# Pinning the first layer's matmuls in traced order, and maxima two to three plan steps behind their VectorE part

## The chip, the cores and the metric

The kernel runs on one core of one Trainium2 chip. The metric is the device time of one execution in microseconds, the median of several runs. Beside the runs stands one profiled execution, from which all rows below are taken.

## The reference

Chunked attention feeds two expert layers. In float32:

```python
# attention: 4 batches x 8 heads x 768 positions x 64; chunks of 32 queries see
# 16 positions to the left, 8 to the right and 8 memory slots (64 keys in all)
scores = scale * np.matmul(q_c, k_full.transpose(0, 1, 3, 2))
a = np.exp(scores - np.max(scores, axis=-1, keepdims=True))
a = a / (np.sum(a, axis=-1, keepdims=True) + 1e-09)
out[:, :, c_start:c_end] = np.matmul(a, v_full)
...
x = np.ascontiguousarray(attn_out.transpose(0, 2, 1, 3)).reshape(B * S, H * D)   # 3072 x 512
h = x @ w_in                                        # first layer: 512 -> 2048
g = np.maximum(h, 0.0) + alpha * np.minimum(h, 0.0)
x = g @ w_out                                       # 2048 -> 512
h = x @ w2_in                                       # second layer
return (h * (1.0 / (1.0 + np.exp(-1.702 * h)))) @ w2_out
```

## The kernel before

**Numbers.** Each float32 operand is scaled by a power of two and split into a high and a low half of 16 bits. A product is three matmuls (high x high, high x low, low x high). The scales come from absolute maxima. `all_max` takes a column of maxima per partition, spreads it over the partitions with a float32 matmul against the identity (the tile `mx`, L119), and reduces the result on DVE (`ar`, L120).

**First layer.** The 3072 tokens are 12 blocks of 256 (b0 to b11). The 2048 hidden units are 8 pairs of 128. A `step` handles one block and one pair: `mlp_g1` issues 24 matmuls into the tile `h` (L575) from the block's input `xt`; `mlp_act` makes the leaky ReLU of it with ACT (`t`, L610) and DVE (`gf`, L613); `mlp_split` makes the 16-bit halves `g` (L127 on ACT, L130 on DVE); four steps later `mlp_g2` issues 24 matmuls into `acc` (L655). There are 96 steps, and 4 more steps of filling. Between the parts of a step `run_plan` carries out what a table of times has due: three plan steps are one step of the layer.

**Attention.** The attention of block b is planned ahead of the steps of that block, from a list `ATT` with offsets. Its matmuls are QK0 and QK1 (`att_qk`, 16 matmuls each, L477 and L478, into the three banks `sps`), and PV0 and PV1 (`att_pv`, 48 small matmuls each, L543, into banks 0 and 1 of `sps`). QK1 overwrites what QK0 wrote once ACT has copied it out (`att_ext`, L494). After PV0, ACT casts the high half of `xt` out of the bank (`att_xhi`, L127) and DVE the low half (`att_xlo`, L130), and the same after PV1. When q, k and v are loaded, ACT takes the absolute maxima of k and q (`att_max`; the tile `junk`, L326), and DVE that of v. In the text, "PV1 of b10" is the one of the attention of block 10.

**Second layer.** Its weights are prepared in the same plan (`w_max`, `w_all`, `w_scale`, `w_dec_a`, ...), its inputs by `y_evac`, `y_max`, `y_unit`. It runs from about 720 us on.

**Order.** The program's trace is a list of instructions in the order of the code. A scheduler with a timeline of its own then decides, for each engine, in which order that engine's queue holds them, within their dependencies. An engine starts its instructions in the order of its queue. A call `tc.keep_in_program_order(x)` ties x behind the instruction traced before it on its engine. Before the change it is used for two instructions of each attention block only (the split of v, L127 and L130).

Of the kernel before, what the change touches and what calls it, by code (L numbers as in the profile page):

```python
# [36 lines left out]
def kernel(  # L37
# [14 lines left out]
    nc = tc.nc  # L52
# [60 lines left out]

    def all_max(m):
        n = m.shape[1]
        r = sm_p.tile([128, 4], F32, tag="ar", name="ar")[:, 0:n]
        pt = ps.tile([128, n, 128], F32, tag="b", name="mx")
        for i in range(n):
            nc.tensor.matmul(out=pt[:, i], lhsT=m[:, i:i + 1].to_broadcast([128, 128]), rhs=eye, start=True, stop=True)  # L119
        nc.vector.tensor_reduce(out=r, in_=pt, axis=AX.X, op=ALU.max, apply_absolute_value=True)  # L120
        return r

    def absmax(o, i):
        nc.vector.tensor_reduce(out=o, in_=i, axis=AX.X, op=ALU.max, apply_absolute_value=True)  # L124
# [17 lines left out]
    wtmp = {}  # L142
# [139 lines left out]
    def bs(nb, i):  # L282
        return blk[nb][:, i:i + 1]
# [187 lines left out]
    def att_qk(nb, i):  # L471
        q1, q2 = att["q", nb]
        kt = att["k", nb]
        k0 = 0 if i == 0 else NM + 128
        for h in range(H):
            o = sps[:, h // 3, h % 3 * TW:h % 3 * TW + TW]
            nc.tensor.matmul(out=o, lhsT=q1[:, i, h], rhs=kt[:, h, k0:k0 + TW], start=True, stop=False)  # L477
            nc.tensor.matmul(out=o, lhsT=q2[:, i, h], rhs=kt[:, h, k0:k0 + TW], start=False, stop=True)  # L478

    def att_ext(nb, i):  # L480
        sc = at_p.tile([128, 9, SL], F32, tag="sc", name="sc", bufs=2)
# [51 lines left out]
    def att_pv(nb, i):  # L533
        aT = att.pop(("a", nb, i))
        if i == 0:
            xt[nb] = xt_p.tile([128, 2, KT, TB], F16, tag="xt", name="xt")
        xp = sps[:, i].rearrange("p (j t) -> p j t", j=HP)
        for j in range(HP):
            for c in range(4):
                o = xp[:, j, 32 * c:32 * c + 32]  # L540
                w = vbd[:, 4 * i + c, j].rearrange("p a (d t) -> p (a d) t", t=2)
                for n, (wt, a) in enumerate(((0, 0), (1, 0), (0, 1))):
                    nc.tensor.matmul(out=o, lhsT=w[:, :, wt], rhs=aT[:, a, j, 32 * c:32 * c + 32], start=(n == 0), stop=(n == 2))  # L543
        att["xp", nb, i] = xp

    def att_xhi(nb, i):
# [19 lines left out]
    def mlp_g1(layer, b, p):  # L566
        x = xt[b]
        hp = ps.tile([128, 2, TB], F32, tag="b", name="h")
        for e in range(2):
            w, c = wslot[p], e  # L570
            n = 0
            for (wt, xh) in TRI:
                for kk in range(KT):
                    o = kk * 256 + c * 128
                    nc.tensor.matmul(out=hp[:, e], lhsT=w[:, wt, o:o + 128], rhs=x[:, xh, kk], start=(n == 0), stop=(n == 3 * KT - 1))  # L575
                    n += 1
        return hp

# [65 lines left out]
    def mlp_g2(layer, b, p):  # L644
        g16 = gt.pop((layer, b, p))
        if layer == 0:
            first = p == 0 or b < NA and p == HF
            last = p == NP - 1 or b < NA and p == HF - 1
            if first:
                acc[layer, b] = [ps.tile([128, 512], F32, tag="b", name="acc") for _ in range(2)]  # L650
            for e in range(2):
                w = wslot[NP + p][:, :, e * 512:(e + 1) * 512]
                for dt in range(KT):
                    for n, (wt, gh) in enumerate(TRI):
                        nc.tensor.matmul(  # L655
                            out=acc[layer, b][dt // 2][:, dt % 2 * TB:(dt % 2 + 1) * TB],
                            lhsT=w[:, wt, dt * 128:(dt + 1) * 128],
                            rhs=g16[:, gh, e],
                            start=(first and e == 0 and n == 0 and dt % 2 == 0),
                            stop=(last and e == 1 and n == 2 and dt % 2 == 1),  # L660
                        )
        else:
            if p == 0:
                acc[layer, b] = [lazy["ps"].tile([128, 512], F32, tag="a", name="acc") for _ in range(3)] + [ps.tile([128, 512], F32, tag="b", name="acc")]
            lazy["left"] += 1 - lazy.pop(("side", b, p))
            w = w2o[p // 2]
            for bank, i, (gs, o) in WIN7:
                for n, (gh, wt) in enumerate(TRI):
                    nc.tensor.matmul(  # L669
                        out=acc[layer, b][bank][:, i * 256:(i + 1) * 256],  # L670
                        lhsT=g16[:, gh, gs],
                        rhs=w[:, o, wt, p % 2],
                        start=(p == 0 and n == 0 and i == 0),
                        stop=(p == NP - 1 and n == 2 and (i == 1 or bank == 3)),
                    )
# [148 lines left out]
    def at(t, fn, *a):  # L824
        plan.setdefault(t, []).append((fn, a))
# [25 lines left out]
    def split(m, p):  # L851
# [6 lines left out]
        (-89.08, alpha_prep), (-85.94, att_qk32, 0, 0), (-84.86, w_load, 0, 0), (-82.33, att_v32, 0, 1),  # L858
        (-78.47, w_load, 1, 0), (-74.28, w_max, 0, 0), (-68.89, att_ext, 0, 0), (-58.71, att_qk32, 0, 1),
        (-54.62, att_ext, 0, 1), (-47.58, att_smax, 0, 0), (-45.32, att_exp, 0, 0), (-41.66, att_sum, 0, 0),  # L860
        (-34.37, w_all, 0, 0, 1), (-33.6, w_max, 0, 1), (-31.58, w_scale, 0, 0, 1), (-28.74, att_v32, 0, 0),
        (-28.07, att_load, 1, 1), (-27.6, att_smax, 0, 1), (-26.72, w_all, 0, 1, 2), (-25.47, att_exp, 0, 1),
        (-25.16, att_ta32, 0, 0), (-24.86, w_load, 0, 4), (-23.18, w_dec_a, 0, 0), (-23.15, w_load, 1, 1),
        (-22.75, w_dec_b, 0, 0), (-22.72, w_split_a, 0, 0), (-22.23, w_scale, 0, 1, 2), (-22.07, w_load, 1, 2),
        (-21.79, att_sum, 0, 1), (-21.75, att_pv32, 0, 0), (-20.45, att_t32, 1), (-19.95, att_ta32, 0, 1),
        (-19.78, att_pv32, 0, 1), (-19.6, att_xmax, 0, 1), (-19.14, w_load, 0, 2), (-19.11, w_load, 1, 3),
        (-18.22, att_v32, 1, 1), (-17.8, w_dec_a, 0, 1), (-16.85, w_max, 0, 2), (-16.78, w_load, 0, 3),
        (-16.05, w_max, 1, 3), (-15.51, w_max, 0, 3), (-14.02, att_xmax, 0, 0), (-13.25, att_load, 2, 2),
        (-13.14, att_v32, 1, 0), (-12.97, w_all, 0, 2, 4), (-11.75, w_load, 0, 5), (-11.41, att_xall, 0),
# [20 lines left out]
        (14.26, att_smax, 2, 0), (14.44, w_dec_b, 1, 3), (14.78, att_vr, 2, 7), (14.88, w_max, 0, 5),  # L890
        (15.48, att_exp, 2, 0), (15.76, w_max, 0, 7), (16.07, w_split_a, 1, 1), (16.29, att_qk, 2, 1),
        (16.29, att_sum, 2, 0), (17.48, att_ext, 2, 1), (18.83, w_split_b, 1, 1), (18.86, att_smax, 2, 1),
        (18.99, att_vr, 2, 5), (19.25, w_all, 0, 4, 6), (19.27, w_split_a, 1, 0), (20.02, w_max, 1, 5),
        (20.61, w_split_a, 1, 2), (20.77, att_vr, 2, 6), (21.27, w_scale, 0, 4, 6), (21.31, att_vr, 2, 4),
        (22.18, att_vr, 2, 3), (23.01, att_vr, 2, 0), (23.08, w_max, 1, 7), (23.28, att_exp, 2, 1),
        (23.31, att_a16, 2, 0), (23.39, w_dec_a, 0, 4), (23.91, w_split_a, 1, 3), (24.32, att_sum, 2, 1),
        (24.48, w_dec_a, 0, 5), (24.64, w_all, 0, 6, 8), (24.68, w_split_b, 1, 3), (24.91, w_dec_b, 0, 4),
# [16 lines left out]
    for g in range(NP):  # L914
# [164 lines left out]
```

## Time and profile before

| | |
|---|---|
| runs | 1191.53, 1194.05, 1190.81 us; median 1191.53 |
| profiled execution | 1190.76 us |
| its span, first to last instruction | 1189.0 us |
| mean granted clock of TensorE | 0.954 |
| busy: PE, DVE, ACT, POOL | 91%, 72%, 53%, 54% of the span |

The profiled execution lasts 1.76 us longer than its span, and 0.77 us less than the median of the runs. PE is TensorE's matmuls; PEld its weight loads, which run beside them. Times of the trace count from the start of the span. A matmul row's duration runs to its modelled end, so that consecutive groups overlap a little: the next group starts before the last one's end.

### The profile page before, as it was taken

To read this page: it belongs to the slowest core of one execution; us is meant where nothing else is said; L and a number is where in the kernel's file an instruction comes from. 1 tells how busy PE (TensorE), PEld (TensorE's weight loads), DVE (VectorE), ACT (ScalarE), POOL (GpSimd) and SP (SyncE) were. 2 spreads that over 40 slices of the span, in tenths; PEclk is the share of its full clock that TensorE was granted. 3 is DMA by queue.
4 is the path that set the end of the run, shared out by engine and by line. 5 is a ranking of instruction groups with operands and counts; after the bars stand their busy time and mean duration, and the time that the engine had idled before them with its cause. 6 is when DMAs were issued, how large, how long until landed. Compare 5 with 4: busy or idle time off the path is not lost.

```text
span 1189.0 us, 25654 instructions
## 1 busy us (share of the span) xinstructions
PE 1078.8 (91%) x10294; PEld 956.7 (80%) x10294; DVE 854.6 (72%) x1509; ACT 632.8 (53%) x968; POOL 637.4 (54%) x740
## 2 busy tenths in 40 slices
PE   3676779988999887999899999989999999999998
PEld 3665668877888776887788988878888888888887
DVE  6898985659787777858698634787676767667662
ACT  4567555556766475756665632545444444443442
POOL 1244542318756456617562811787685676666672
PEclk8678889999899999999899999999999999999999
DMA  9969227576989678887965390640110202000001
GB/s 207 305 126 192 90 72 160 91 145 181 238 207 262 137 203 164 235 156 191 186 191 139 102 351 19 266 169 19 56 44 6 76 19 80 21 6 14 19 19 37
DMA packets 250536, 154.53 MB, mean 130 GB/s; under 512 B 201200, under 2 KB 221680, under 8 KB 249392
## 3 DMA queue, kind: packets, MB, share of 16 engines
q1 hardware_dynamic: 250416, 152.88, 50.3%
q8 instruction: 81, 1.33, 0.5%
q14 instruction: 39, 0.32, 0.1%
HBM read 91.96 MB, written 38.93 MB: 110 GB/s over the span
## 4 chain that ended last, share of the span: by engine, by line
PE 51%; DVE 19%; DMA 11%; POOL 5%; issue 5%; ACT 4%; SPq 4%; ACTq 0%; DVEq 0%; POOLq 0%
PE acc L669 17%; PE x L586 16%; PE h L575 8%; PE acc L655 8%; DVE g L130 3%; DVE gf L613 2%; DMA q<-q 2%; POOL ga L620 2%; DMA wbig<-in_moe_w_in_dram 2%; DVE wr L198 1%; DVE wmax L124 1%; DMA w<-in_moe_w_in_dram 1%; DVE wr L199 1%; DVE blk L124 1%; DMA vbd<-in_v_dram 1%
## 5 line engine op out<-in xcount | busy, mean ns | idle before, releaser
L620 POOL TENSOR_TENSOR ga<-ga 128x128 f32<-128x128 f32 x384 | 213.1, 579 | 170.7 <-DVE ga L618 158.6
L575 PE MATMUL h<-xt,wbig 128*128 128x256 f16 x2304 | 279.6, 279 | 22.8 <-ACT xt L127 17.0
L655 PE MATMUL acc<-g,wbig 128*128 128x256 f16 x2304 | 280.5, 280 | 8.9 <-DVE yf L685 4.0
L575 PEld LDWEIGHTS <-wbig 128*128 128x128 f16 x2304 | 230.4, 100 | 55.4 <-issue 24.5
L655 PEld LDWEIGHTS <-wbig 128*128 128x128 f16 x2304 | 229.7, 100 | 41.5 <-issue 8.9
L669 PE MATMUL acc<-w2o,g 128*128 128x256 f16 x2016 | 231.7, 274 | 4.0 <-ACT g L127 3.6
L586 PE MATMUL x<-yt,w2i 128*128 128x256 f16 x2016 | 229.9, 273 | 1.0 <-DVE ha L596 0.9
L669 PEld LDWEIGHTS <-g 128*128 128x128 f16 x2016 | 197.7, 98 | 28.9 <-ACT g L127 4.5
L586 PEld LDWEIGHTS <-w2i 128*128 128x128 f16 x2016 | 197.3, 98 | 24.2 <-issue 1.4
L130 DVE SCALAR_TENSOR_TENSOR g<-ga,gk,g 128x896 f16<-128x896 f32 x96 | 121.0, 1266 | 91.2 <-ACT g L127 90.9
L127 ACT ACTIVATE g<-ga,gk 128x896 f16<-128x896 f32 x96 | 99.0, 1038 | 96.0 <-POOL ga L620 87.0
L613 DVE SCALAR_TENSOR_TENSOR gf<-t,oma,h 128x256 f32<-128x256 f32 x192 | 83.5, 473 | 76.9 <-ACT t L610 76.9
L130 DVE SCALAR_TENSOR_TENSOR g<-gf,gk,g 128x512 f16<-128x512 f32 x81 | 80.5, 994 | 20.2 <-ACT g L127 20.0
L610 ACT ACTIVATE t<-h 128x512 f32<-128x512 f32 x96 | 56.7, 591 | 70.0 <-PE h L575 46.3
L803 POOL TENSOR_TENSOR o<-o 128x256 f32<-128x256 f32 x77 | 74.3, 979 | 10.0 <-ACT o L798 9.5
L617 ACT ACTIVATE ga<-ha,l2t 128x512 f32<-128x512 f32 x48 | 34.5, 718 | 80.7 <-DVE ha L598 80.7
L228 POOL TENSOR_TENSOR wt<-wr 128x512 f32<-128x512 f32 x16 | 24.0, 1499 | 81.1 <-DVE wr L205 81.0
L214 POOL TENSOR_TENSOR wbig<-wr,wbig 128x1024 f16<-128x1024 f32 x16 | 35.1, 2202 | 53.4 <-ACT wbig L209 53.4
L127 ACT ACTIVATE g<-gf,gk 128x512 f16<-128x512 f32 x81 | 57.7, 712 | 0.5 <-DVE gf L613 0.4
L494 ACT COPY sc<-sps 32x504 f32<-32x504 f32 (+2 forms) x112 | 56.2, 502 | 1.0
L618 DVE SCALAR_TENSOR_TENSOR ga<-ga,ha 128x512 f32<-128x512 f32 x48 | 35.6, 741 | 21.0 <-ACT ga L617 21.0
L543 PE MATMUL sps<-aT,vbd 128*128 128x32 f16 x960 | 27.5, 179 | 22.7 <-DVE xt L130 16.3
(194 smaller groups left out, 1514.7 us busy)
## 6 DMA issues: line engine op xcount, KB each, us to landing
yt_dr<-yh SPq DMA_DIRECT2D x42, 256.0 KB
yt<-yt_dr SPq DMA_DIRECT2D x42, 256.0 KB
w<-in_moe_w_in_dram SPq DMA_DIRECT2D x10, 1024.0 KB
w<-in_moe_w_out_dram SPq DMA_DIRECT2D x10, 1024.0 KB
vbd<-v_dr SPq DMA_DIRECT2D x80, 112.0 KB
w2i_dr<-wh SPq DMA_DIRECT2D x28, 256.0 KB
w2o_dr<-wh SPq DMA_DIRECT2D x28, 256.0 KB
w2i<-w2i_dr SPq DMA_DIRECT2D x4, 1792.0 KB
```

Of the source, the lines that this page charges most:

```text
L127: return nc.scalar.activation(out=hi, in_=src, func=ACTF.Copy, scale=s)
L130: return nc.vector.scalar_tensor_tensor(out=lo, in0=src, scalar=s, in1=hi, op0=ALU.mult, op1=ALU.subtract)
L494: nc.scalar.copy(d[32 * c:32 * c + 32, ..., 0:WIN], x[32 * c:32 * c + 32, ..., bo + CH * c:bo + CH * c + WIN])
L575: nc.tensor.matmul(out=hp[:, e], lhsT=w[:, wt, o:o + 128], rhs=x[:, xh, kk], start=(n == 0), stop=(n == 3 * KT - 1))
L586: nc.tensor.matmul(out=xs[bank][:, i], lhsT=w[:, o, wt, kk * 256 + c:kk * 256 + c + 128], rhs=yt[sb, yi][:, yh, kk], start=(n == 0), stop= ...
L610: nc.scalar.activation(out=t, in_=hp, func=ACTF.Relu, scale=-1.0)
L613: nc.vector.scalar_tensor_tensor(out=g[:, e], in0=t[:, e], scalar=oma[:, f:f + 1], in1=hp[:, e], op0=ALU.mult, op1=ALU.add)
L618: nc.vector.scalar_tensor_tensor(out=t, in0=t, scalar=1.0, in1=hp, op0=ALU.add, op1=ALU.mult)
L620: nc.gpsimd.tensor_tensor(out=g[:, out_], in0=g[:, x], in1=g[:, y], op=op)
L655: nc.tensor.matmul(out=acc[layer, b][dt // 2][:, dt % 2 * TB:(dt % 2 + 1) * TB], lhsT=w[:, wt, dt * 128:(dt + 1) * 128], rhs=g16[:, gh, e] ...
L669: nc.tensor.matmul(out=acc[layer, b][bank][:, i * 256:(i + 1) * 256], lhsT=g16[:, gh, gs], rhs=w[:, o, wt, p % 2], start=(p == 0 and n == ...
L803: e.tensor_tensor(out=ov[:, out_], in0=ov[:, x], in1=ov[:, y], op=op)
```

## The change

From the 20th step of the first layer on, a flag `pin` is set, and a helper `keep` ties each matmul of the first layer to the instruction traced before it on PE: those of `all_max`, `att_qk`, `att_pv`, `mlp_g1` and `mlp_g2` of layer 0. The matmul part of two maxima becomes a plan entry of its own: `w_mx` stands two plan steps behind `w_all` (and `w_scale` moves by two), `y_mx` 2.5 behind `y_max` (and `y_unit` moves by one). In the table for the start of the program `w_mx` stands directly behind each `w_all`.

```diff
+    pin = [False]
+
+    def keep(x):
+        return tc.keep_in_program_order(x) if pin[0] else x
...
-            nc.tensor.matmul(out=pt[:, i], lhsT=m[:, i:i + 1].to_broadcast([128, 128]), rhs=eye, start=True, stop=True)
+            keep(nc.tensor.matmul(out=pt[:, i], lhsT=m[:, i:i + 1].to_broadcast([128, 128]), rhs=eye, start=True, stop=True))
...
-        wtmp["r", m, a] = all_max(r)
+        wtmp["q", m, a] = r
+
+    def w_mx(m, a):
+        wtmp["r", m, a] = all_max(wtmp.pop(("q", m, a)))
...
-            nc.tensor.matmul(out=o, lhsT=q1[:, i, h], rhs=kt[:, h, k0:k0 + TW], start=True, stop=False)
-            nc.tensor.matmul(out=o, lhsT=q2[:, i, h], rhs=kt[:, h, k0:k0 + TW], start=False, stop=True)
+            keep(nc.tensor.matmul(out=o, lhsT=q1[:, i, h], rhs=kt[:, h, k0:k0 + TW], start=True, stop=False))
+            keep(nc.tensor.matmul(out=o, lhsT=q2[:, i, h], rhs=kt[:, h, k0:k0 + TW], start=False, stop=True))
...
-                    nc.tensor.matmul(out=o, lhsT=w[:, :, wt], rhs=aT[:, a, j, 32 * c:32 * c + 32], start=(n == 0), stop=(n == 2))
+                    keep(nc.tensor.matmul(out=o, lhsT=w[:, :, wt], rhs=aT[:, a, j, 32 * c:32 * c + 32], start=(n == 0), stop=(n == 2)))
...
-                    nc.tensor.matmul(out=hp[:, e], lhsT=w[:, wt, o:o + 128], rhs=x[:, xh, kk], start=(n == 0), stop=(n == 3 * KT - 1))
+                    keep(nc.tensor.matmul(out=hp[:, e], lhsT=w[:, wt, o:o + 128], rhs=x[:, xh, kk], start=(n == 0), stop=(n == 3 * KT - 1)))
...
+    def y_mx(b):
         yf["r", b] = all_max(bs(b, 10))
...
         at(t + 7, w_all, m, p, p + 1)
-        at(t + 9, w_scale, m, p, p + 1)
+        at(t + 9, w_mx, m, p)
+        at(t + 11, w_scale, m, p, p + 1)
...
         at(t + 4, y_max, b)
-        at(t + 7, y_unit, b)
+        at(t + 6.5, y_mx, b)
+        at(t + 8, y_unit, b)
...
     for s in range(STEPS + EX):
+        pin[0] = s >= 20
         step(s)
+    pin[0] = False
```

The matmuls of `acc` for layer 0 are wrapped in the same way. No instruction is added or removed. The change moves them on every engine from about 228 us on, at two places above all.

The first is PE at PV1 of b10. Here `g_7965` is the input of the acc group between PV0 and PV1. Before, 11 of the 24 h matmuls stand ahead of PV1:

```order
L655 LDWEIGHTS wbig
L655 MATMUL acc<-g_7965,wbig 128x256
L575 LDWEIGHTS wbig
L575 MATMUL h<-xt,wbig 128x256
...
L575 MATMUL h<-xt,wbig 128x256
L543 LDWEIGHTS vbd
L543 MATMUL sps<-aT,vbd 128x32
```

Now, with the line numbers of the changed kernel (543 is 551, 575 is 583, 655 is 663):

```order
L663 LDWEIGHTS wbig
L663 MATMUL acc<-g_7965,wbig 128x256
L551 LDWEIGHTS vbd
L551 MATMUL sps<-aT,vbd 128x32
...
L551 MATMUL sps<-aT,vbd 128x32
L583 LDWEIGHTS wbig
L583 MATMUL h<-xt,wbig 128x256
```

PV1 stands directly behind the acc group, and the whole h group behind PV1. It is so in b3 to b11 now. Before, 11 to 13 h matmuls stood there in b3, b5, b6, b8, b10 and b11; in b4 it was the whole h group of 24, and in b7 and b9 the h group and 5 acc matmuls.

The second is ACT around the same place of b7 (`xt` the two halves of the block's input, `t`, `v_...`, `g_...` work of the layer and of v, `junk` the maxima of the next k and q, `yh` casts for the second layer). Before:

```order
L127 ACTIVATE xt<-sps 128x4x128
L754 CAST yh<-yf 128x512
L754 CAST yh<-t 128x512
L754 CAST yh<-yf 128x512 x2
L610 ACTIVATE t<-h 128x512
L127 ACTIVATE v_5973<-vf,blk_140 128x1536
L127 ACTIVATE g_5976<-gf,gk_145 128x512
L326 ACTIVATE junk,blk_141<-kf 128x1536
L127 ACTIVATE xt<-sps 128x4x128
L326 ACTIVATE junk,blk_141<-qf 128x1024
```

Now (127 is 132, 326 is 334, 610 is 618, 754 is 764):

```order
L132 ACTIVATE xt<-sps 128x4x128
L764 CAST yh<-yf 128x512
L764 CAST yh<-t 128x512
L764 CAST yh<-yf 128x512 x2
L132 ACTIVATE xt<-sps 128x4x128
L334 ACTIVATE junk,blk_141<-kf 128x1536
L618 ACTIVATE t<-h 128x512
L132 ACTIVATE v_5969<-vf,blk_140 128x1536
L132 ACTIVATE g_5972<-gf,gk_145 128x512
L334 ACTIVATE junk,blk_141<-qf 128x1024
```

The second xt now stands ahead of the junk of k, and t, v and g stand behind that junk. b9 is changed in the same way. The matmuls for maxima move on PE too: that of the second layer's weights (tile `wa`) stands one h group later, that for y one acc group later.

## Rows read from the trace of the kernel before

**Rows 1.** The page's head: span, and busy time of each engine.

```profile
span 1189.0 us, 25654 instructions
...
PE 1078.8 (91%) x10294; PEld 956.7 (80%) x10294; DVE 854.6 (72%) x1509; ACT 632.8 (53%) x968; POOL 637.4 (54%) x740
```

**Rows 2.** Windows: PE, PEld, DVE, ACT, POOL busy (instructions), granted clock, DMA, GB/s.

```profile
222.30:656.60 434.30, 394.16 (x4132) 349.30 (x4131) 333.67 (x599) 268.58 (x420) 230.17 (x185) 0.96 0.78 183
656.60:720.00 63.40, 63.40 (x657) 57.12 (x655) 29.51 (x57) 27.87 (x47) 26.68 (x23) 1.00 0.59 212
...
610.40:656.60 46.20, 43.57 (x476) 39.13 (x475) 37.71 (x78) 26.33 (x41) 19.95 (x16) 0.96 0.50 120
```

**Rows 3.** Waits of PE, 172 to 720 us: total, times, longest.

```profile
PE sps L543 <- DVE xt L130: 16.3, 5, 4.1
PE sps L477 <- ACT sc L494: 7.2, 4, 2.4
PE sps L543 <- DMA aT<-a: 5.7, 2, 4.6
...
PE h L575 <- ACT xt L127: 3.7, 2, 2.1
...
PE mx L119 <- DVE ar L120: 0.5, 1, 0.5
```

**Rows 4.** Timeline of PE, b10: start, duration, instruction [idle before, releaser].

```profile
622.94 2.78 PE L655 MATMUL acc<-g,wbig 128*128 128x256 f16 x24
625.56 1.36 PE L575 MATMUL h<-xt,wbig 128*128 128x256 f16 x11
629.56 1.44 PE L543 MATMUL sps<-aT,vbd 128*128 128x32 f16 x48 [2.63 <-DVE xt L130]
630.84 2.53 PE L575 MATMUL h<-xt,wbig 128*128 128x256 f16 x13
```

**Rows 5.** Timeline of PE, PV1 of b4, b6 (two rows), b7 and b9.

```profile
299.42 1.46 PE L543 MATMUL sps<-aT,vbd 128*128 128x32 f16 x48 [4.58 <-DMA aT<-a]
...
406.21 1.35 PE L543 MATMUL sps<-aT,vbd 128*128 128x32 f16 x48 [3.94 <-DVE xt L130]
407.41 2.84 PE L575 MATMUL h<-xt,wbig 128*128 128x256 f16 x13
...
465.85 1.44 PE L543 MATMUL sps<-aT,vbd 128*128 128x32 f16 x48 [3.76 <-DVE xt L130]
...
576.27 1.44 PE L543 MATMUL sps<-aT,vbd 128*128 128x32 f16 x48 [4.13 <-DVE xt L130]
```

**Rows 6.** Timeline of PE, first matmul of QK1 behind b5, b6 and b8.

```profile
372.13 0.23 PE L477 MATMUL sps<-kt,q 128*128 128x160 f16 x1 [2.42 <-ACT sc L494]
...
429.21 0.23 PE L477 MATMUL sps<-kt,q 128*128 128x160 f16 x1 [1.50 <-ACT sc L494]
...
540.02 0.23 PE L477 MATMUL sps<-kt,q 128*128 128x160 f16 x1 [2.44 <-ACT sc L494]
```

**Rows 7.** Timeline of PE, b7 and b9 after PV1.

```profile
467.13 3.12 PE L655 MATMUL acc<-g,wbig 128*128 128x256 f16 x19
...
475.44 1.54 PE L575 MATMUL h<-xt,wbig 128*128 128x256 f16 x8 [2.12 <-ACT xt L127]
...
577.54 4.21 PE L655 MATMUL acc<-g,wbig 128*128 128x256 f16 x19
...
586.41 1.03 PE L575 MATMUL h<-xt,wbig 128*128 128x256 f16 x8 [1.60 <-ACT xt L127]
```

**Rows 8.** Timeline of ACT, b6 (first row) and b7.

```profile
418.93 1.48 ACT L326 ACTIVATE junk<-kf 128x1536 f16<-128x1536 f32 x1 [5.47 <-DMA qf<-in_q_dram]
...
473.32 1.48 ACT L326 ACTIVATE junk<-kf 128x1536 f16<-128x1536 f32 x1 [3.33 <-DMA kf<-in_mem_k_dram]
...
474.81 0.58 ACT L127 ACTIVATE xt<-sps 128x512 f16<-128x512 f32 x1
```

**Rows 9.** Timeline of DVE behind a maximum's scales, b6.

```profile
422.40 0.87 DVE L613 SCALAR_TENSOR_TENSOR gf<-t,oma,h 128x256 f32<-128x256 f32 x2 [5.29 <-ACT t L610]
```

More of the change, by code (lines that the diff above doesn't have):

```diff
@@ L654, in mlp_g2 @@
                     for n, (wt, gh) in enumerate(TRI):
-                        nc.tensor.matmul(
+                        keep(nc.tensor.matmul(
                             out=acc[layer, b][dt // 2][:, dt % 2 * TB:(dt % 2 + 1) * TB],
@@ L660, in mlp_g2 @@
                             stop=(last and e == 1 and n == 2 and dt % 2 == 1),
-                        )
+                        ))
         else:
@@ L860 @@
         (-54.62, att_ext, 0, 1), (-47.58, att_smax, 0, 0), (-45.32, att_exp, 0, 0), (-41.66, att_sum, 0, 0),
-        (-34.37, w_all, 0, 0, 1), (-33.6, w_max, 0, 1), (-31.58, w_scale, 0, 0, 1), (-28.74, att_v32, 0, 0),
-        (-28.07, att_load, 1, 1), (-27.6, att_smax, 0, 1), (-26.72, w_all, 0, 1, 2), (-25.47, att_exp, 0, 1),
+        (-34.37, w_all, 0, 0, 1), (-34.37, w_mx, 0, 0), (-33.6, w_max, 0, 1), (-31.58, w_scale, 0, 0, 1), (-28.74, att_v32, 0, 0),
+        (-28.07, att_load, 1, 1), (-27.6, att_smax, 0, 1), (-26.72, w_all, 0, 1, 2), (-26.72, w_mx, 0, 1), (-25.47, att_exp, 0, 1),
         (-25.16, att_ta32, 0, 0), (-24.86, w_load, 0, 4), (-23.18, w_dec_a, 0, 0), (-23.15, w_load, 1, 1),
@@ L868 @@
         (-16.05, w_max, 1, 3), (-15.51, w_max, 0, 3), (-14.02, att_xmax, 0, 0), (-13.25, att_load, 2, 2),
-        (-13.14, att_v32, 1, 0), (-12.97, w_all, 0, 2, 4), (-11.75, w_load, 0, 5), (-11.41, att_xall, 0),
+        (-13.14, att_v32, 1, 0), (-12.97, w_all, 0, 2, 4), (-12.97, w_mx, 0, 2), (-11.75, w_load, 0, 5), (-11.41, att_xall, 0),
         (-10.4, att_xs, 0), (-9.99, w_scale, 0, 2, 4), (-9.05, att_xhi, 0, 0), (-8.93, att_xlo, 0, 0),
@@ L892 @@
         (16.29, att_sum, 2, 0), (17.48, att_ext, 2, 1), (18.83, w_split_b, 1, 1), (18.86, att_smax, 2, 1),
-        (18.99, att_vr, 2, 5), (19.25, w_all, 0, 4, 6), (19.27, w_split_a, 1, 0), (20.02, w_max, 1, 5),
+        (18.99, att_vr, 2, 5), (19.25, w_all, 0, 4, 6), (19.25, w_mx, 0, 4), (19.27, w_split_a, 1, 0), (20.02, w_max, 1, 5),
         (20.61, w_split_a, 1, 2), (20.77, att_vr, 2, 6), (21.27, w_scale, 0, 4, 6), (21.31, att_vr, 2, 4),
@@ L896 @@
         (23.31, att_a16, 2, 0), (23.39, w_dec_a, 0, 4), (23.91, w_split_a, 1, 3), (24.32, att_sum, 2, 1),
-        (24.48, w_dec_a, 0, 5), (24.64, w_all, 0, 6, 8), (24.68, w_split_b, 1, 3), (24.91, w_dec_b, 0, 4),
+        (24.48, w_dec_a, 0, 5), (24.64, w_all, 0, 6, 8), (24.64, w_mx, 0, 6), (24.68, w_split_b, 1, 3), (24.91, w_dec_b, 0, 4),
         (25.09, att_vr, 2, 2), (25.62, w_split_b, 1, 0), (26.74, att_ta, 2, 0), (26.89, w_scale, 0, 6, 8),
```

## The prediction

> **What bounds the kernel now.** I read the page's head first: TensorE (PE) is busy 91% of the span, VectorE (DVE) 72%, ScalarE (ACT) 53% [rows 1]. That average hides two regimes, so the windows come next. From 222.3 to 656.6 us, where seven blocks of attention run beside the first layer and where the matmul order changes, PE is busy 394.16 of 434.30 us: 40 us of waiting. From 656.6 to 720 us, once the last attention block is nearly through, it is busy 63.40 of 63.40 us [rows 2]. So a delay that reaches 656.6 us is not made good afterwards, while one inside the earlier stretch can vanish in a later wait that something else sets.
>
> Which waits these are is in PE's list of waits [rows 3]. PV1, the second half of the attention-times-V product (L543), waits for DVE's xt of the first half in five blocks, 16.3 us in all, and for the transposed weights aT by DMA in two, 5.7 us. QK1 (L477) waits for ACT's copies out of the score bank four times, 7.2 us. The h matmuls (L575) of a new block wait for ACT's xt twice, 3.7 us. The diff touches the order around each of these.
>
> **Cost of one matmul.** In block 10 the 24 acc matmuls start at 622.94 us and the next group at 625.56 [rows 4]: 2.62/24 = 0.109 us each. A group of 24 lasts 2.78 us to its last end, so one of 11 should last 1.36, which the row shows, one of 13 about 1.58 and one of 19 about 2.23.
>
> **PV1 loses cover (b5, b6, b8, b10).** Before, 11 h matmuls (b5: 13) stand between the acc group and PV1; pinned, PV1 stands straight behind the acc group and all 24 h behind it. PV1 cannot start before xt of the first half is written, and the order of ACT and DVE ahead of that xt has nothing in it that waits for the moved h. So PV1 starts when it did, and 11 x 0.109 = 1.20 us of matmuls that filled its wait now come after it. In b10: PE is idle from 625.6 instead of from 626.9 us, PV1 still starts at 629.56 [rows 4], and the acc group behind the h comes 1.20 us later.
>
> Is this given back? In b10 not: in 610.4 to 656.6 us PE's idle time is 46.20 - 43.57 = 2.63 us, exactly PV1's own wait [rows 2, 4], and none follows it. In the other blocks it mostly is. QK1 waited 2.42, 1.50 and 2.44 us at 372, 429 and 540 us [rows 6], in the blocks after PV1 of b5, b6 and b8. What ends these waits is ACT, whose copies stand in its queue behind the absolute maxima "junk", and those wait for loads: at 418.93 us ACT had been idle 5.47 us for a DMA [rows 8]. A PE that is 1.2 us later finds those copies at the same time; its QK1 wait shrinks by 1.2. That is my choice; if the copies moved with PE, each block would keep its 1.20. In b3 and b11, which lose 11 to 13 matmuls of cover too, PV1 waited for nothing (the list has seven waits of PV1, of b4 to b10): bounds 0 and 1.3 each, I take 0.
>
> **The longer wait is colder.** After PV1's wait of 2.63 us in b10 the next 13 h lasted 2.53 us instead of 1.58: 0.95 lost [rows 4]. After 3.94 us in b6 the same 13 lasted 2.84: 1.26 lost; after 4.13 us in b9 the 19 acc lasted 4.21 instead of 2.23: 1.98 lost [rows 5, 7]. The granted clock of the stretch is 0.96 against 1.00 behind it [rows 2]. In b10 the wait becomes 2.63 + 1.20 = 3.83 us, nearest to b6's 3.94: 1.26 - 0.95 = 0.3 us more. Bounds: 0, and 1.98 - 0.95 = 1.0.
>
> **b7 and b9: one long wait for two.** Before, 29 matmuls (24 h, 5 acc) stand between the acc group and PV1, which still waits 3.76 and 4.13 us [rows 5]; later the new block's h wait 2.12 and 1.60 us for ACT's xt [rows 7]. In b7 that xt (474.81 us) stands in ACT's queue behind the junk that waited 3.33 us for a load, until 473.32 [rows 8], though PV1 had written its bank seven us before. In the new order ACT takes that xt ahead of this junk, so the second wait goes. The price: all 29 matmuls stand behind PV1, which adds 29 x 0.109 = 3.16 us to its wait. Per block: +3.16 - 2.12 = +1.0 and +3.16 - 1.60 = +1.6, before the clock. Against this: the acc matmuls at 467.13 and 577.54 ran cold in front of a second wait; with one wait the engine warms once, worth up to the 1.98 us of b9. Bounds -0.9 to +3.2 per block; I take 0, as the two halves of the argument are nearly equal and QK1's wait in the block behind b9 (the remaining 7.2 - 2.42 - 1.50 - 2.44 = 0.84 us) takes up some.
>
> **b4.** The 24 h ahead of PV1 go behind it: its wait, 4.58 us for aT [rows 5], grows to 7.2, +2.6. Behind it b5's own PV1 waited another 1.8 us for DVE (16.3 less the other four) and QK1 after that 2.42 us for ACT, neither of which hangs on PE: absorbed. I take 0; bounds 0 and +2.6.
>
> **The maxima (mx).** all_max moves two to three plan steps behind its VectorE part, so that PE, pinned, meets it later: one h group later for the weights' maxima, one acc group for y's. Cost bound 2.62 us of lateness each. Who waits: DVE's reduction ar and, behind it, the weight scales. DVE there has idle time of 5.29 us in front of gf for another reason [rows 9], and the weights' decoding has many steps until it is used. I cost it 0. A maximum that is met too early would hold all of PE, but mx waited next to nothing before, so nothing is gained either.
>
> **Sum.** b10: +1.20 + 0.3 = +1.5; b5, b6, b8: 3 x 1.20 less the same at QK1 = 0; b7, b9, b4, mx: 0. Against the profiled execution: 1190.76 + 1.5 = 1192.3 us. That execution lies 0.77 under the median of the runs, 1191.53, so the forecast is **1193.0 us**. Its own range takes b7 and b9 at -0.9 each with b10 at +0.3 (1190.0), and at the other end +1.0 each with b10's 2.2 (1195.7).
>
> **The rivals.**
>
> *A, faster: the fixed order fills better.* The two h waits, 3.7 us [rows 3], vanish and PV1 is not later, because the 29 matmuls behind it run at full clock, saving the 1.98 us as well: 1191.5 - 5.7 = 1185.8 us. For it: ACT's order does free xt, and PE is ahead in stretches where 40 us are idle. Against it: PV1's wait is set by DVE, which the pin does not speed up. It decides if xt of the first half comes at least 3.2 us earlier in b7 and b9, for instance because DVE and ACT, too, have fewer misordered pieces ahead of it. 0.27.
>
> *B, slower: the lost cover adds up.* Mechanism: no later wait absorbs it, since PE's delay moves the next QK, the copies behind it and so the next block's whole attention chain. Price: 4 x 1.20 + 2 x 3.16 + 2.62 = 13.7 us, less the 3.7 of the h waits: +10.0, 1201.5 us. For it: PV1's wait is the largest on the list, and the change lengthens it in seven blocks. Against it: QK1's waits end with ACT behind a load, which does not hang on PE. It decides from the point where QK1's waits stay at 1.5 to 2.4 us though PE comes later. 0.30. The Trainium skill, TensorE: Matmul & The Clock Gate, section "HAM oscillation — how this bites in real kernels", speaks for this rival: waits between bursts of matmuls send the clock to its lower level, so that each burst starts cold, and seven longer waits would be worse than shorter ones. The trace agrees that bursts behind a wait run slower (0.95 to 1.98 us lost, above); by the rule alone each of seven blocks would lose up to 1.0 more than I take, some 7 us, and land near 1200 us.
>
> *C, no change in time at all:* the attention chain over DVE, ACT and the loads sets everything up to 629.5 us, and there xt comes earlier by the 1.2 us that b10 loses. 1191.5 us. It lies in the same case as the forecast, and cannot be told from it by the time alone.
>
> **The numbers.** Forecast with C 0.43, A 0.27, B 0.30. About 0.3%, 3.6 us, can be told from no change: 1187.9 to 1195.1. A lies below it, the forecast in it, B above. To leave no more than 2 in 10 out, the range runs from a little under A's 1185.8 to a little over B's price: 1184.5 to 1202.0.
>
> **What would show it.** After: PV1 of b10 waits 3.8 us instead of 2.63, for the same DVE xt, and nothing idles from there to the end of the layer. The waits of L543 for DVE's xt grow from 16.3 to about 26 us. Those of QK1 shrink to 2 to 4 us and those of h for ACT's xt go to 0. The second layer takes as long as before. Wrong would be: waits of PV1 that stay near 16 us with the h waits gone (A), QK1 waits that stay at 7 us while those of PV1 grow (B), or a new wait, of acc for g or of DVE for mx, in the list.

## The result

The changed kernel takes 1209.61 us (median of 4 runs, 1208.36 to 1210.97), the kernel before 1192.79 us (4 runs, 1190.81 to 1194.72). The ratio is 1.0141, with a 95% interval of 1.0117 to 1.0166: slower by 1.4%, some 17 us. The forecast was 1193.0 us, its range 1184.5 to 1202.0 us. The result lies above the range and on the side of rival B, beyond that rival's own price.

### The profile page after: what moved, and what is told of

The parts are those of the page before. It is cut to its first block, busy times and chain, and to the rows that moved or that the text cites. A ratio compares the mean times of both kernels' runs of the same rounds, so it can differ in the third digit from the quotient of the medians.

```text
span 1208.8 us, 25639 instructions
## 1 busy us (share of the span) xinstructions
PE 1076.0 (89%) x10294; PEld 954.3 (79%) x10294; DVE 851.3 (70%) x1509; ACT 632.3 (52%) x968; POOL 637.2 (53%) x740
## 4 chain that ended last, share of the span: by engine, by line
PE 42%; DVE 9%; DMA 5%; POOL 4%; ACT 2%; SPq 2%; issue 2%; ACTq 0%; DVEq 0%; POOLq 0%
PE acc L677 17%; PE x L594 16%; PE h L583 4%; PE acc L663 4%; DVE g L135 2%; POOL ga L628 2%; DVE gf L621 1%; DMA w<-in_moe_w_out_dram 1%; DMA v_dr<-v 1%; DMA w<-in_moe_w_in_dram 1%; DVE wmax L129 1%; DVE q L135 1%; DVE blk L129 1%; POOL yh L765 1%; POOL wh L247 1%
## 5 line engine op out<-in xcount | busy, mean ns | idle before, releaser
L583 PE MATMUL h<-xt,wbig 128*128 128x256 f16 x2304 | 286.5, 284 | 17.1 <-ACT xt L132 12.5
L663 PE MATMUL acc<-g,wbig 128*128 128x256 f16 x2304 | 270.2, 274 | 15.7 <-DVE yf L693 5.5
L663 PEld LDWEIGHTS <-wbig 128*128 128x128 f16 x2304 | 224.7, 98 | 44.3 <-issue 11.5
L135 DVE SCALAR_TENSOR_TENSOR g<-gf,gk,g 128x512 f16<-128x512 f32 x81 | 81.4, 1004 | 19.5 <-ACT g L132 19.5
L551 PE MATMUL sps<-aT,vbd 128*128 128x32 f16 x960 | 27.6, 180 | 45.2 <-DVE xt L135 33.5
L551 PEld LDWEIGHTS <-vbd 128*128 128x128 f16 x960 | 27.4, 99 | 47.6 <-issue 25.5
```

What stands on the lines that cost most here:

```text
L135: return nc.vector.scalar_tensor_tensor(out=lo, in0=src, scalar=s, in1=hi, op0=ALU.mult, op1=ALU.subtract)
L551: keep(nc.tensor.matmul(out=o, lhsT=w[:, :, wt], rhs=aT[:, a, j, 32 * c:32 * c + 32], start=(n == 0), stop=(n == 2)))
L583: keep(nc.tensor.matmul(out=hp[:, e], lhsT=w[:, wt, o:o + 128], rhs=x[:, xh, kk], start=(n == 0), stop=(n == 3 * KT - 1)))
L663: keep(nc.tensor.matmul(out=acc[layer, b][dt // 2][:, dt % 2 * TB:(dt % 2 + 1) * TB], lhsT=w[:, wt, dt * 128:(dt + 1) * 128], rhs=g16[:, g ...
```

## The profile after

The page's head of the changed kernel, which answers to [rows 1]:

```profile
span 1208.8 us, 25639 instructions
...
PE 1076.0 (89%) x10294; PEld 954.3 (79%) x10294; DVE 851.3 (70%) x1509; ACT 632.3 (52%) x968; POOL 637.2 (53%) x740
```

No engine has more work than before; PE even has 2.8 us less. The 19.8 us by which the span grew are waits of PE, not work. The windows that answer to the first two of [rows 2], cut at the same matmuls:

```profile
223.60:672.90 449.30, 389.01 (x4132) 346.56 (x4131) 325.83 (x595) 268.55 (x421) 228.22 (x183) 0.94 0.77 177
672.90:739.75 66.85, 65.25 (x657) 57.98 (x656) 31.51 (x59) 27.02 (x46) 28.05 (x25) 0.97 0.55 201
```

The stretch with attention lasts 449.30 us instead of 434.30, the one behind it 66.85 instead of 63.40. PE's idle time in the first is 449.30 - 389.01 = 60.3 us; it was 40.1. Which waits these are is in PE's list, 172 to 740 us, as in [rows 3] (total, times, longest):

```profile
PE sps L551 <- DVE xt L135: 33.5, 6, 8.0
PE sps L551 <- DMA aT<-a: 8.6, 1, 8.6
PE acc L663 <- DVE yf L693: 5.5, 2, 5.0
PE acc L663 <- DVE gf L621: 5.1, 6, 1.5
PE sps L485 <- ACT sc L502: 4.8, 4, 1.5
PE sps L551 <- DVE pf L114: 2.4, 1, 2.4
```

PV1 (L551) waits 33.5 + 8.6 + 2.4 = 44.5 us where it waited 22.0. QK1 (L485) gave back 2.4 us, 4.8 instead of 7.2. The waits of h for xt are gone. And acc now waits for DVE's gf, 5.1 us, which was 0.9 us before: the new wait, of acc for g's input, that the prediction named as a sign of being wrong. Four of the PV1 and the h groups behind them (b7, b8, b9 and b11), in the timeline of PE:

```profile
471.62 1.44 PE L551 MATMUL sps<-aT,vbd 128*128 128x32 f16 x48 [7.12 <-DVE xt L135]
472.90 3.51 PE L583 MATMUL h<-xt,wbig 128*128 128x256 f16 x24
...
528.92 1.45 PE L551 MATMUL sps<-aT,vbd 128*128 128x32 f16 x48 [5.44 <-DVE xt L135]
530.20 3.86 PE L583 MATMUL h<-xt,wbig 128*128 128x256 f16 x24
...
589.04 1.44 PE L551 MATMUL sps<-aT,vbd 128*128 128x32 f16 x48 [7.95 <-DVE xt L135]
590.32 4.51 PE L583 MATMUL h<-xt,wbig 128*128 128x256 f16 x24
...
694.45 1.35 PE L551 MATMUL sps<-aT,vbd 128*128 128x32 f16 x48 [1.60 <-DVE xt L135]
695.65 4.45 PE L583 MATMUL h<-xt,wbig 128*128 128x256 f16 x24
```

The waits in b7 and b9 are 3.4 and 3.8 us longer than in [rows 5], a little over the 3.16 us of cover that was counted. b11, which waited for nothing before, waits 1.60 us, and its 24 h last 4.45 us instead of 2.78: 3.3 us together, nearly all of the 3.45 us by which the second window grew.

How the delay builds up is seen from the starts of PV0, less those of the kernel before, in the timelines of three kernels (the two others are experiments, below):

| PV0 of | b4 | b5 | b6 | b7 | b8 | b9 | b10 | b11 |
|---|---|---|---|---|---|---|---|---|
| changed kernel | 2.2 | 6.7 | 5.6 | 5.6 | 8.1 | 12.1 | 13.4 | 16.3 |
| pinned in b4, b7, b9 only | 0.3 | 1.7 | 0.8 | 1.3 | 7.2 | 10.8 | 10.1 | 13.2 |
| pinned in b5, b6, b8, b10 only | 0.6 | 0.0 | 3.0 | 2.9 | 3.2 | 2.9 | 1.8 | 3.5 |

The delay is not even. It comes in steps behind b4, b7, b8 and b10, and some of what one block loses the next gives back.

## The experiments

Each kernel was timed against the kernel before in the same job; the ratio to it is given with its 95% interval.

**The pin alone.** The changed kernel with the maxima back at their old plan steps (`all_max` within `w_all` and `y_max` again):

```diff
-        at(t + 9, w_mx, m, p)
-        at(t + 11, w_scale, m, p, p + 1)
+        at(t + 9, w_scale, m, p, p + 1)
...
-        at(t + 6.5, y_mx, b)
-        at(t + 8, y_unit, b)
+        at(t + 7, y_unit, b)
```

> Pinned as in the change, but the maxima stay at their old plan steps; on PE only PV1 stands elsewhere than before (ahead of all 24 h). Theory 1, the cover lost by PV1 costs the time: PV1's waits grow to about 40 us in all and the time is 1203 to 1211 us. Theory 2, the later maxima delay the casts and with them everything behind: 1190 to 1197 us, PV1's waits under 28 us. A sum of both would lie between, 1197 to 1203.

Measured: 1205.98 us against 1192.03, ratio 1.0118 (1.0090 to 1.0147). **The maxima alone**, pin off:

```diff
-        pin[0] = s >= 20
+        pin[0] = False
```

> The maxima at their new plan steps, nothing pinned; PV1 keeps 11 to 24 h ahead of it. Theory 1: 1189 to 1196 us, PV1's waits about 22 us in all as before. Theory 2: 1203 to 1211 us, with the first xt later behind PV0 as in the changed kernel (9 us in b8 instead of 5).

Measured: 1196.23 us against 1192.03, ratio 1.0032 (1.0017 to 1.0048). The pin costs some 14 us, the moved maxima some 4. Together they make some 18 us, the whole change (16.8) within the intervals. The pin is the larger part, and the maxima, which the prediction had at 0, are not free.

**Which maxima.** Those of the weights alone, nothing pinned:

```diff
-        at(t + 6.5, y_mx, b)
-        at(t + 8, y_unit, b)
+        at(t + 4, y_mx, b)
+        at(t + 7, y_unit, b)
```

> Nothing pinned, only the weights' maxima moved by two plan steps, those of y where they were. If the weights' maxima carry what the move of both costs (4 us): 1195 to 1199 us. If those of y, which stand ahead of PV0 and feed casts on ACT ahead of xt, carry it: 1190 to 1195 us.

Measured: 1194.38 us against 1192.85, ratio 1.0015 (0.9997 to 1.0032). This does not tell the two apart: its interval reaches from no change to most of the 4 us.

**Which blocks.** The pin alone, only in the steps around PV1 of some blocks. PE's order is that of the pinned kernel at these blocks and that of the kernel before at the others.

```diff
-        pin[0] = s >= 20
+        pin[0] = s in [8 * b + i for b in (4, 7, 9) for i in range(1, 6)]
```

> Pinned only in the steps around PV1 of b4, b7 and b9, maxima at their old plan steps; there PV1 goes ahead of the 24 to 29 matmuls, while b5, b6, b8 and b10 keep their 11 to 13 h. The prediction's terms for these blocks (0 each, up to 2.6 and 3.2): 1191 to 1197 us. If lost cover is paid in full there: 24 and twice 29 matmuls less the h waits, 2.6 + 6.3 - 3.7 = 5.2 us, 1196 to 1200 us. If all of the pin's loss comes from these blocks: 1203 to 1209 us.

Measured: 1204.55 us against 1192.85, ratio 1.0113 (1.0097 to 1.0129).

> Pinned only around PV1 of b5, b6, b8 and b10, maxima at their old plan steps; b4, b7 and b9 keep their order. The prediction's terms (0, 0, 0 and 1.5): 1191 to 1196 us. Cover paid in full: 4 x 1.2 = 4.8 us, 1196 to 1200 us. If all of the pin's loss comes from these blocks: 1203 to 1209 us. If the two runs add up to the 14 us of the pin, the blocks' losses are separate; if not, they hang on each other.

Measured: 1193.86 us against 1192.85, ratio 1.0013 (0.9998 to 1.0027). (The table's timelines are single executions, 13.2 and 3.5 us longer than that of before; the medians count.) The two add up, 11.7 + 1.0 = 12.7 us, to the 14 of the pin within the intervals, and nearly all of it comes with the pin in b4, b7 and b9, where the kernel before had 24 to 29 matmuls ahead of PV1. In the four blocks where 11 to 13 matmuls moved, the loss is next to nothing.

The traces show that these two kernels differ in more than the number of matmuls. In the first, ACT and DVE start their instructions in the order of the kernel with every block pinned, in all of b3 to b10 and but for one instruction a block, though PE is pinned in three blocks only. In b8, where PE's order is that of the kernel before, ACT's g stands behind the junk of k, which waits 6.61 us for a load (g at 538.48 us); before, g stood ahead of it (523.03). In the second, PE has the pinned order in its four blocks, while ACT and DVE keep the order of the kernel before but for one instruction a block from b6 on, and for up to five in b4 and b5. So the loss goes with the new orders of ACT and DVE and with the 24 to 29 matmuls of three blocks; 11 to 13 matmuls of lost cover in four blocks, without those orders, cost 1.0 us.

**One block by itself.** The pin alone, from the 80th step on:

```diff
-        pin[0] = s >= 20
+        pin[0] = s >= 80
```

> Pinned from the 80th step on only, maxima at their old plan steps: all engines' orders are those of the kernel before up to b10, and only PV1 of b10 and b11 moves ahead of its 11 to 12 h. The prediction's own term for b10: +1.2 to +2.2 us, 1193 to 1196 us. If a block's loss is what the pin of all blocks showed for b10 (5.6 us with the maxima at their old steps) and does not hang on the blocks ahead of it: 1197 to 1200 us.

Measured: 1195.20 us against 1192.81, ratio 1.0022 (1.0010 to 1.0034). The timeline of its PE at PV1 of b10:

```profile
629.76 1.37 PE L548 MATMUL sps<-aT,vbd 128*128 128x32 f16 x48 [3.25 <-DVE xt L135]
630.97 4.38 PE L580 MATMUL h<-xt,wbig 128*128 128x256 f16 x24
```

The wait is 3.25 us instead of 2.63, and the 24 h behind it last 4.38 us, 1.60 more than at full clock (before: 0.95 lost). The wait grew by 0.62 us where the prediction has 1.20, the loss behind it by 0.65 where it has 0.3; the sum, 1.3 us, lies at the lower end of its term for b10, +1.2 to +2.2 us. The median of all runs is 2.4 us up.

**PV1 behind all of h.** The changed kernel with PV1 and the xt behind it one plan step later:

```diff
-        ... (34, att_pv, 1), (35, att_xhi, 1), (36, att_xlo, 1),
+        ... (35, att_pv, 1), (36, att_xhi, 1), (37, att_xlo, 1),
```

> The changed kernel with PV1 and its xt one plan step later, so that the whole h group stands ahead of PV1 again; all else pinned. Theory 1: each block gets back 2.6 us of cover where the change took 1.2 to 3.2, and the time is 1186 to 1195 us. Theory 2: PV1's waits shrink by the cover but the time stays at 1203 or more, since the casts still come late.

Measured: 1207.83 us against 1192.03, ratio 1.0137 (1.0115 to 1.0160). The list of PE's waits, same stretch as above:

```profile
PE h L583 <- ACT xt L132: 18.9, 6, 6.7
PE sps L551 <- DVE xt L135: 13.4, 6, 4.4
PE h L583 <- DVE xt L135: 11.0, 5, 3.0
```

PV1's waits fell to 13.4 us, and 29.9 us of waits stand at the first h of the new block, which needs the xt that PV1 makes ([rows 3] have 3.7 there). Cover taken from behind PV1 is missed there. Theory 1 in its simple form, that each matmul of cover ahead of PV1 is a gain, falls.

**PV1 in the middle of h.** `mlp_g1` issues PV1 between its two halves:

```diff
         for e in range(2):
+            if e == 1 and s in mid:
+                att_pv(mid[s], 1)
             w, c = wslot[p], e
...
+        mid[8 * nb + 3] = nb
```

> The changed kernel with PV1 between the two halves of the h group: 12 h ahead of it, 12 behind, all pinned, as the kernel before has it in b5, b6, b8 and b10. Both theories: 1.2 to 1.3 us a block come back, 8 to 10 us in all, 1198 to 1203 us. If PV1's place is not the cause: 1206 us or more.

Measured: 1200.84 us against 1192.99, ratio 1.0071 (1.0047 to 1.0094): 9 us of the 17 come back. The same with the maxima at their old steps:

> The same place of PV1, pinned, with the maxima at their old plan steps. If PV1's place is the cause of what the pin costs, 1193 to 1199 us; what stays above the kernel before is then b4, b7 and b9, where before has the whole h group and more ahead of PV1. If not: 1204 us or more.

Measured: 1202.38 us against 1192.99, ratio 1.0080 (1.0060 to 1.0100): only 4 us under the pin alone. Twelve matmuls ahead of PV1 are better than none or 24, but what they are worth hangs on the other orders, which the moved maxima change too.

**No wait for xt at all.** PV1 into a PSUM tile of its own, first in the changed kernel, then in the kernel before:

```diff
-        xp = sps[:, i].rearrange("p (j t) -> p j t", j=HP)
+        xp = sps[:, i].rearrange("p (j t) -> p j t", j=HP) if i == 0 else ps.tile([128, HP, 128], F32, tag="b", name="xp")
```

> The changed kernel with PV1 writing a PSUM tile of its own, so that it no longer waits for the first half's xt; it stands where the change puts it. Theory 1: the waits of PV1 for xt are gone, those for aT by DMA may appear, and the time falls to 1182 to 1195 us. Theory 2: xt and the casts are still late, and the wait moves to the h of the new block: 1203 us or more.

Measured: 1200.90 us against 1192.03, ratio 1.0084 (1.0055 to 1.0113).

> The kernel before, nothing pinned, with PV1 in a PSUM tile of its own, so that it does not wait for the first half's xt. If what PV1 waits for is the cost, 1178 to 1189 us and a version better than both. If another wait takes its place (QK for ACT's copies, h for xt), 1190 to 1200 us.

Measured: 1201.54 us against 1192.81, ratio 1.0075 (1.0055 to 1.0094), slower by 9 us than the kernel before, though PV1 waits for no xt. The list of PE's waits of this one:

```profile
PE sps L477 <- ACT sc L494: 12.8, 3, 4.7
PE xp L543 <- DMA aT<-a: 9.2, 2, 4.6
PE h L575 <- DVE gf L613: 8.6, 3, 4.2
PE acc L655 <- DVE yf L685: 5.5, 2, 5.2
```

The 16.3 us of PV1 behind DVE are gone; QK1 waits 5.6 us longer than in [rows 3], h waits 8.6 us for gf (the tile comes from the pool that holds h), and the aT wait grew. This does not show that PV1's wait cost nothing before: the edit changed ACT's order, too. In b7 and b9 t, v and g now stand behind the junk of k, as in the changed kernel, though nothing is pinned; in b7 that junk waits 6.83 us for its load, and t starts at 475.98 us, 9.1 us later than before.

**The split of v.** In the changed kernel ACT's cast of v comes later behind PV0 in b4 to b9 (17.0 us on average against 11.5 before), and DVE's half of the split too (20.5 against 15.3). The chain of waits runs through it to the next load of v. Theory 3 said that this is the cause. The edit moves the cast one plan step ahead:

```diff
-        (14, att_hi, 2), (15, att_lo, 2), (16, att_vw), (13, att_swap),
+        (13, att_swap), (13, att_hi, 2), (14, att_lo, 2), (15, att_vw),
```

> The changed kernel with the split of the next v one plan step earlier; the order of PE is that of the changed kernel, matmul for matmul, and on ACT the cast of v stands ahead of the t that needs the h group behind PV1. Theory 3, PV1 ahead of h costs time because that t, and behind it the cast of v that starts the next block's attention, come later on ACT (in b4 to b9 40 us after PV1's start in sum, 13 before): 1192 to 1202 us. Theory 1, PE's lost cover itself: no change, 1206 to 1212 us.

Measured: 1207.16 us against 1193.01, ratio 1.0123 (1.0103 to 1.0143).

The same edit with the pin alone, the maxima at their old steps:

> Pinned, maxima at their old plan steps, and the split of v one plan step earlier. Theory 3: 1187 to 1197 us, some 4 us under the same edit with the maxima moved. Theory 1: about 1206 us as without the edit.

Measured: 1212.01 us, ratio 1.0163 (1.0146 to 1.0180).

The same edit in the kernel before:

> The kernel before with the split of v one plan step earlier, nothing pinned. Theory 3: the cast of v, which came up to 4.6 us after PV1 in b5, b6, b8 and b10, comes earlier there: 1180 to 1191 us. Theory 1: no change, 1189 to 1196 us.

Measured: 1197.25 us, ratio 1.0032 (1.0017 to 1.0047), slower.

And the kernel before with the split later, `(16, att_hi, 2), (16.5, att_lo, 2), (16.9, att_vw)`:

> The kernel before with the split of v two plan steps later, nothing pinned: the suspected harm without the pin. Theory 3: 1197 to 1210 us, according to how much later the cast starts. Theory 1: within 4 us of the kernel before, since PV1 keeps its 11 to 29 matmuls of cover.

Measured: 1207.65 us, ratio 1.0124 (1.0104 to 1.0143). A later v is dear even with nothing pinned, but an earlier one is no gain in any kernel. Since DVE's half had come only 3 us earlier in the first of these (17.5 us behind PV0), theory 4 put both halves ahead of t (`(13, att_hi, 2), (13.2, att_lo, 2), (13.4, att_vw)`):

> The changed kernel with both halves of the next v's split, ACT's cast and DVE's subtraction, ahead of the t and gf of the h group behind PV1; PE's order is that of the changed kernel. Theory 4: the loop that binds runs from DVE's half of v's split over the stores and the next load of v to v's maximum and the next PV0; the pin moved that half from 15.3 to 20.5 us behind PV0 on average, and the ACT half alone (the earlier run) left it at 17.5. If it comes at 16 us or less, the time is 1194 to 1203 us. Theory 1, cover alone: 1205 to 1212 us.

Measured: 1209.60 us against 1192.99, ratio 1.0141 (1.0120 to 1.0163). DVE's half now came 12.2 us behind PV0, and nothing was won. The first line of its waits of PE:

```profile
PE sps L551 <- DVE xt L135: 43.1, 9, 6.8
```

PV1 waits as long as in the changed kernel. The steps behind b7 and b9 are gone (PV0 of b8 is 9.5 us late after 14.2 for b7, that of b10 14.4 after 17.4 for b9); larger ones stand behind b5 and b8 (5.7 and 7.9 us). The same edit with PV1 in the middle of h, and with the tile of its own:

> The changed kernel with PV1 between the halves of h and both halves of v's split early. Two loops, PE's through PV1 and the one through v's split and load, take turns: with both relieved 1190 to 1197 us. If the loop through v binds nothing: 1199 to 1203 us, as with PV1 in the middle alone.

Measured: 1198.98 us against 1192.81, ratio 1.0056 (1.0034 to 1.0077), against 1200.84 without the edit.

> The changed kernel with PV1 in a PSUM tile of its own and both halves of v's split early. Two loops: PV1 waits for nothing on DVE and v's load comes early, 1186 to 1195 us. If the loop through v binds nothing: 1199 to 1203 us, as with the tile alone.

Measured: 1198.89 us, ratio 1.0055 (1.0036 to 1.0073), against 1200.90. Neither differs beyond its interval. Theories 3 and 4 fall in this form: an earlier v does not give the time of the pin back. No version beat the kernel before.

**All eighteen, by ACT's order.** In ten of the eighteen kernels, as in the changed one, the t of the h group at PV1 stands behind the junk of k in both b7 and b9. These ten are 6.1 to 19.0 us slower than the kernel before. Of the eight others, five are 1.0 to 4.2 us slower; three, in which v's split was put late, or all of it early in the changed kernel, or PV1 and its xt later, are 14.6 to 16.6 us slower. So that place of t goes with a loss, but it is not the only source of one.

## Why the prediction was wrong

**b5, b6, b8, b10: right.** The step "PV1 loses cover" had 0, 0, 0 and +1.5 us; pinned alone, these four cost 1.0 us (-0.2 to 3.2). That QK1 gives the cover back is in the rows of this kernel, 2.7 us of QK1 waits for ACT against 7.2 in [rows 3]:

```profile
PE sps L482 <- ACT sc L499: 2.7, 3, 1.2
```

PV1 of b10 waits 3.84 us in this kernel, 3.83 was forecast, and b10 by itself cost about its term, as shown above. "PV1 starts when it did" holds for b6, b8 and b10; in b5 PV1 comes 9.4 us behind PV0, 7.2 before, and the blocks behind give that back.

**b4, b7 and b9: the step that failed.** "One long wait for two" netted 29 matmuls of cover against the h waits that vanish and took 0, and b4 was taken as absorbed. Measured: 11.7 us, where the three upper bounds together are 2.6 + 3.2 + 3.2 = 9.0. The netting itself was right: in the kernel pinned there alone PV1's waits grew from 22.0 to 30.3 us, the h waits went, and PE came out of b7 and b9 no later than it went in (below). What failed is the list of prices. It has only the 29 matmuls; what the new order of ACT puts behind the junk in place of xt is not on it and so was taken as 0. That price stands at other lines: QK1's waits stayed, and acc waited 5.0 us for gf, 0.9 before. The list of its waits:

```profile
PE sps L548 <- DVE xt L135: 23.1, 6, 6.9
PE sps L482 <- ACT sc L499: 7.9, 4, 5.0
PE sps L548 <- DMA aT<-a: 7.2, 1, 7.2
PE acc L660 <- DVE gf L618: 5.0, 3, 3.7
```

Where the larger part arises can be followed in b7 and b8 of this kernel. Its PV1 of b7 is only 1.3 us later than before, but PV0 of b8 is 7.2 us later (table). First ACT in the kernel before, two rows ahead of the junk at 473.32 of [rows 8]:

```profile
466.88 0.59 ACT L610 ACTIVATE t<-h 128x512 f32<-128x512 f32 x1
467.37 2.06 ACT L127 ACTIVATE v<-vf,blk 128x1536 f16<-128x1536 f32 x1
```

Then ACT in the kernel pinned in b4, b7 and b9:

```profile
474.27 1.48 ACT L331 ACTIVATE junk<-kf 128x1536 f16<-128x1536 f32 x1 [5.09 <-DMA qf<-in_q_dram]
...
475.75 0.58 ACT L615 ACTIVATE t<-h 128x512 f32<-128x512 f32 x1
476.23 2.06 ACT L132 ACTIVATE v<-vf,blk 128x1536 f16<-128x1536 f32 x1
```

The h group of this t now stands behind PV1, and t stands behind the junk of k, which waits for its load. t and the cast of v start 8.9 us later. The order of ACT that the front part shows had exactly this; the prediction read from it only that xt leaves its place behind the junk, and did not ask what takes that place. What follows on DVE and PE of the same kernel:

```profile
476.37 0.88 DVE L618 SCALAR_TENSOR_TENSOR gf<-t,oma,h 128x256 f32<-128x256 f32 x2 [6.46 <-ACT t L615]
...
479.75 1.94 DVE L135 SCALAR_TENSOR_TENSOR v<-vf,blk,v 128x1536 f16<-128x1536 f32 x1
...
496.58 1.75 DVE L129 TENSOR_REDUCE blk<-vf 128x1 f32<-128x1536 f32 x1 [2.90 <-DMA vf<-in_mem_v_dram]
...
504.30 0.86 DVE L618 SCALAR_TENSOR_TENSOR gf<-t,oma,h 128x256 f32<-128x256 f32 x2
```

```profile
505.22 5.30 PE L660 MATMUL acc<-g,wbig 128*128 128x256 f16 x24 [3.73 <-DVE gf L618]
...
518.61 1.35 PE L548 MATMUL sps<-aT,vbd 128*128 128x32 f16 x48
```

DVE idles 6.46 us for t. The split of v is late, so the next v is loaded late, and DVE, in the order of its queue, waits 2.90 us for that load with the gf of the layer behind it. PE then waits 3.73 us for gf, and its matmuls run cold: 24 acc take 5.30 us. How little of this is lost cover is seen at the first mx of b8's stretch, the same matmul by count in both kernels, in PE's rows of the kernel before and of this one:

```profile
500.05 0.83 PE L119 MATMUL mx<-eye,blk 128*128 128x128 f32 x6
```

```profile
500.66 0.83 PE L124 MATMUL mx<-eye,blk 128*128 128x128 f32 x6
```

PE is 0.6 us late there and was 1.3 late at PV0 of b7, ahead of the pinned PV1: the 29 matmuls have been given back. The next h group starts 7.0 us late (510.31 against 503.34 us), and the 6.4 us between are the wait for gf and the cold acc behind it. At b9 it is the same: 10.8 us late at PV0, 8.5 at the mx behind it. One block later than the edit, on a line that the prediction did not look at, lies time that it did not count.

The next step of this kernel, 3.6 us from PV0 of b8 to that of b9, follows ACT's g behind the junk in b8: DVE idles 7.36 us for that g and splits v behind it at 539.88 us; its gf comes at 545.22, ACT's t waits 2.09 us for that, and the copies for which QK1 waits 5.0 us, until 549.78, stand behind t.

The path is shown for these two steps of this kernel, 9.5 of its 13.2 us; the 3.1 us behind b10 were not followed. It is not shown to be the whole cause in the changed kernel. There acc's longest wait for gf is 1.5 us and the step behind b7 2.5 us, while those behind b4 and b8 are 4.5 and 4.0. With both halves of v's split early the steps behind b7 and b9 went, but others came and the time stayed. With PV1 in the middle of h 9 us came back though the cast of v in b7 and b9 was as late as in the changed kernel (20.5 and 19.5 us behind PV0 against 20.1 and 19.9). To keep the junk behind t and v on ACT with PE pinned, which would be the direct test, was not tried.

**The maxima: 0 was wrong, and no one size replaces it.** Moved alone they cost 4.2 us (2.0 to 5.7). The step looked at what waits for the scales. In the changed kernel b11 shows one thing that was missed: y's maxima come an acc group later, and the casts that need them stand on ACT ahead of t and of xt, so that PV1 waits 1.60 us. With the pin alone b11 costs next to nothing (its PV0 starts 16.1 us late and its whole span is 16.5 us longer), with the maxima moved 3.3 us, as the second window shows. But the 4.2 us of the maxima alone do not arise there: in that kernel PV0 of b11 is 5.2 us late and the span 5.2 us longer. And in two pairs above the moved maxima were the faster: 1200.84 against 1202.38 us with PV1 in the middle, within the intervals, and 1207.16 against 1212.01 us with v's split early, beyond them. How much each of the two maxima carries was not resolved.

**The sum.** 11.7 (b4, b7, b9) + 1.0 (b5, b6, b8, b10) + 4.2 (maxima) = 16.9 us; measured are 16.8. The forecast had 0, 1.5 and 0. The agreement is in part luck: each part is known within some 2 us, the pin in all blocks measured 14 and not 12.7, and the price of the maxima hangs on the order that they are moved in.

**The rivals.** B had the sign, but not the mechanism: "no later wait absorbs it" is wrong of the four blocks, and of b7 and b9 too, where the lost cover was given back. That its price of 1201.5 us, the cover counted in full, lies nearer to the result than the forecast is luck. The sentence on the Trainium skill, TensorE: Matmul & The Clock Gate, section "HAM oscillation — how this bites in real kernels", held for the single wait (0.7 to 1.7 us lost behind each of the four above) but not for the sum: by the prediction's estimate from it seven longer waits would lose some 7 us more to the clock, and PE's busy time for the same 4132 matmuls of the stretch fell by 5.15 us, 389.01 against 394.16, though the granted clock fell from 0.96 to 0.94. The longer waits cost no more clock than the shorter ones. A and C had nothing for them: xt came no earlier. PV1, which waits for it, starts 11.1 and 11.9 us behind PV0 in b7 and b9, 10.9 and 11.3 before.

## What to carry to other kernels

When an order is pinned on one engine, read the new order of every other engine for what now stands behind an instruction that waits for a load, not only for what got free: here the maximum of the next block's k took the place ahead of a small t, and the price appeared a block later as a wait of another line. An edit that takes a wait away does not price that wait as long as the orders of other engines move with it: taking PV1's largest wait away made this kernel 9 us slower, with ACT's order changed in b7 and b9. To see whether a delay was given back, compare the start of the same matmul, by count, in both traces. Where a change touches many places, try it on a part of them: two kernels, each pinned in some of the blocks, showed what no list of waits did.

## What the runs showed that was not expected

The loss behind a wait does not follow the wait's length. The 24 h behind PV1, 2.78 us at full clock, lasted 3.51 us after a wait of 7.12, 3.86 after 5.44, 4.51 after 7.95 and 4.45 after one of 1.60. And nearly every change of the order near this kernel's own, in either direction, cost time: of eighteen kernels none was faster, v's split early cost 4 us and late 15 in the same kernel.
